# Per-head k-by-v products as 64x64 matmuls on the two column halves of the array, with the short chunk filled up by zeros

## The chip, the core and the metric

The kernel runs on one core of one Trainium2 chip. The time is the device time of one execution in microseconds (us); the kernel before was run three times, and one further execution was profiled. PE is TensorE (the matmul engine), PEld its weight loads, DVE the vector engine, ACT the scalar engine, POOL GpSimd, and SP the engine whose queue issues all of this kernel's DMAs.

## What is computed

The program joins linear attention with two feed-forward blocks. Batch is 8, there are 8 heads of width 64 and 576 rows in a sequence, all in float32:

```python
kv  = np.einsum('bhsd,bhse->bhde', k, v)          # 64x64 for each batch and head
out = np.einsum('bhsd,bhde->bhse', q, kv)
out = out / sqrt(mean(out * out, axis=-1) + 1e-6) * g_norm
x   = out, heads side by side                      # 4608 x 512
x   = (s * relu(x @ w_in)**2 + b) @ w_out          # d_ff 2048
y   = max(x @ w1, x @ w2, x @ w3) @ w_out2         # d_ff 768
```

The change concerns only the first line, `kv`.

## The kernel before

Heads are handled in pairs: `p` counts the four pairs of a batch `bb`, so there are 32 products of k by v. A pair's k is 128 columns wide (64 for each head), and so is its v. The 576 rows are cut into four full chunks of 128 rows and one short chunk of 64 (`NC = 4`, `REM = 64`). `s1` multiplies the whole 128x128 k-by-v product for each chunk (L201 for the full ones, L202 for the short one), accumulated in one PSUM tile `kvps`, and then copies only the two 64x64 blocks on the diagonal out, one for each head: by L207 for the first two batches (`EARLY`), by `hilo` (L82 on ACT, L83 on DVE) into `kvbd` for the other six. The operands are plain float32, and the trace shows two weight loads and two matmuls for each matmul call: 256 of L201 for 32 x 4 calls, 64 of L202 for 32.

`load_kv` fetches a pair's four full chunks (`kv`, two buffers in pool `kvp`) and the short one (`kvr`, a single buffer in pool `kvrp`). Batch 0 takes its tiles from the weight pool instead, with one load for the short chunks of all four pairs. Loads run two pairs ahead of `s1` (`kv_ahead`).

After `s1` of a pair come `s2` (the split of q into two float32r parts), `s3` (q times kv, L226 or L231), and `s4` (norm and the writing of the activations `xh`, `xl`). The first feed-forward block (`u1` L313, `u2` L336) runs in 'slots', a column block of 128 of the 2048 at a time for a tile of 512 tokens; the steps `s1` to `s4` of the next tokens are spread evenly between the slots (`todo`, `beside`). Its partial sums go out to DRAM (`y_dr`). The second block (`v1` L377, `v2` L396) follows after all of that. Weights are taken apart on ACT and DVE (`w_float`, `w_parts`), mostly in the first 200 us. A list scheduler turns this program order into the order on each engine.

A few small constants (`g_sb`, `sb_sb`, `lnb`, `exb`) stand in four tiles of their own; L491 to L513 fill them at the start.

Of the kernel before, what the change touches and what calls it, by code (L numbers as in the profile page):

```python
# [7 lines left out]
F32 = mybir.dt.float32  # L8
# [3 lines left out]
ALU = mybir.AluOpType  # L12
# [7 lines left out]
P = 128  # L20
# [3 lines left out]
def fused_kernel(ctx, tc, qt, kv, kvr, g_norm, w_in, w_out, s, b, w1, w2, w3, w_out2, out):  # L24
    nc = tc.nc
    B, NP, SM, _, _ = kv.shape
    REM = kvr.shape[2]
    S = SM + REM
    D = g_norm.shape[0]
# [8 lines left out]
    NC = SM // P  # L38
# [6 lines left out]
    def pool(name, bufs, space=None):  # L45
        kw = {"space": space} if space is not None else {}
        return ctx.enter_context(tc.tile_pool(name=name, bufs=bufs, **kw))

    const = pool("const", 1)
    wp = pool("wp", 2 * KF)  # L50
# [5 lines left out]
    wt1 = pool("wt1", 2)  # L56
    gp1 = pool("gp1", 1)
    kvp = pool("kvp", 2)
    kvr_p = pool("kvrp", 1)
    qp = pool("qp", 2)  # L60
    ap2 = pool("ap2", 2)
    ap1 = pool("ap1", 1)
# [6 lines left out]
    EARLY = 2  # L69
    start = [wp.tile([P, NP + 2, P], F32, tag="w", name=f"start{i}") for i in range(EARLY)]  # L70
    onesf, zero = start[0][:, NP, :], start[0][:, NP + 1, :]
    g_sb = const.tile([P, 1], F32, name="g_sb")
    sb_sb = const.tile([P, 2], F32, name="sb_sb")
    lnb = const.tile([P, 1], F32, name="lnb")
    exb = const.tile([P, 1], F32, name="exb")
    kvbd = [const.tile([P, 2, P], F32R, name=f"kvbd{p}") for p in range(NP)]
    y_dr = [dram.tile([P, KD, TW], F32, name=f"y_dr{t}") for t in range(NTILE)]

    dma = nc.sync.dma_start

    def hilo(hi, lo, src, eng):
        nc.scalar.activation(out=hi, in_=src, func=ACTF.Copy)  # L82
        eng.tensor_tensor(out=lo, in0=src, in1=hi.bitcast(F32), op=ALU.subtract)  # L83


    def w_load(src):
# [18 lines left out]
    def w_parts(bf, nm):  # L105
        t = wp.tile([P, 2, DM], F32R, tag="w", name=nm)
        with tc.high_priority(60):
            hilo(t[:, 0, :], t[:, 1, :], bf, nc.vector)
        return t

    class Weights:
# [11 lines left out]
        def to(self, cnt):  # L123
            cnt = min(cnt, len(self.need))
            while self.done < cnt:
                self.load(self.half + 3)
                if self.half < len(self.need):
                    self.f32[self.half] = w_float(self.raw.pop(self.half))
                    self.half += 1
                if self.done < self.half - 1 or self.half == len(self.need):  # L130
                    _, d, key = self.need[self.done]
                    d[key] = w_parts(self.f32.pop(self.done), f"w{self.done}")
                    self.done += 1
# [4 lines left out]
    def stage():  # L138
        return stp.tile([P, DM], F32, tag="st", name="st")


    kv_t, krem, q_t = {}, {}, {}

    def load_kv(bb, p):
        first = bb == 0
        pl, tg = (wp, "w") if first else (kvp, "kv")
        t = pl.tile([P, NC, 2, P], F32, tag=tg, name="kv")
        dma(out=t, in_=kv[bb, p].rearrange("(p c) z d -> p c z d", c=NC))
        kv_t[bb, p] = t
        if not first:  # L150
            t = kvr_p.tile([REM, 2, P], F32, tag="kvr", name="kvr")
            dma(out=t, in_=kvr[bb, p])
            krem[bb, p] = t
        elif p == 0:
            t = wp.tile([REM, NP, 2, P], F32, tag="w", name="kvr")
            dma(out=t, in_=kvr[0].rearrange("n p z d -> p n z d"))
            for i in range(NP):
                krem[0, i] = t[:, i]

    def load_q(it):  # L160
        bb, pc, p = it
# [13 lines left out]
    def temps(it, nm):  # L175

        n = PIECES[it[0]][it[1]][1] - PIECES[it[0]][it[1]][0]
        if it[0] >= EARLY:
            pl, dt, tg = TEMPS[nm]
            return pl.tile([P, PW], dt, tag=tg, name=nm)[:, :n]  # L180
        return tmp_t[it][:, HEADS[nm], :n]
# [8 lines left out]
    def bank(bb, i, nm):  # L190
        if bb > 0:
            return ps_a.tile([P, TW], F32, tag="a", name=nm)
        pl, tg = ((ps_y, f"y{i % 4}"), (ps_h, "h"), (ps_a, "a"))[("kvps", "ops", "mps").index(nm)]
        return pl.tile([P, TW], F32, tag=tg, name=nm)

    def s1(bb, p):
        t = kv_t.pop((bb, p))
        r = krem.pop((bb, p))
        ps = bank(bb, p, "kvps")
        for c in range(NC):  # L200
            nc.tensor.matmul(ps[:, :P], lhsT=t[:, c, 0, :], rhs=t[:, c, 1, :], start=(c == 0), stop=False)  # L201
        nc.tensor.matmul(ps[:, :P], lhsT=r[:, 0, :], rhs=r[:, 1, :], start=False, stop=True)  # L202
        t = kvbd[p]
        for j in range(2):
            r = slice(j * D, (j + 1) * D)
            if bb < EARLY:
                nc.vector.tensor_copy(start[bb][:, p, :][r, r], ps[r, r])  # L207
                continue
            hilo(t[r, 0, r], t[r, 1, r], ps[r, r], nc.vector)

    qT_t, o_t = {}, {}

    def s2(it):
        if it[0] < EARLY:
            return
        t = q_t.pop(it)
        qh, ql = temps(it, "qh"), temps(it, "ql")
        hilo(qh, ql, t, nc.vector)
        qT_t[it] = (qh, ql)

    def s3(it):
        bb, pc, p = it
        n = PIECES[bb][pc][1] - PIECES[bb][pc][0]
        ps = bank(bb, p, "ops")[:, :n]
        if bb < EARLY:
            nc.tensor.matmul(ps, lhsT=start[bb][:, p, :], rhs=q_t.pop(it), start=True, stop=True)  # L226
        else:
            qh, ql = qT_t.pop(it)
            w = kvbd[p]
            for i, (l, r) in enumerate(((w[:, 0, :], qh), (w[:, 0, :], ql), (w[:, 1, :], qh))):  # L230
                nc.tensor.matmul(ps, lhsT=l, rhs=r, start=(i == 0), stop=(i == 2))  # L231
        sq, og = temps(it, "sq"), temps(it, "og")
        nc.scalar.activation(out=sq, in_=ps, func=ACTF.Square)
        if bb < EARLY:
            if bb == 0:
                nc.scalar.activation(out=og, in_=ps, func=ACTF.Copy, scale=g_sb)
            else:
                nc.vector.tensor_scalar(out=og, in0=ps, scalar1=g_sb, scalar2=None, op0=ALU.mult)
            o_t[it] = (og, sq, None)
            return  # L240
        nc.scalar.activation(out=og, in_=ps, func=ACTF.Copy, scale=g_sb)
        sh, sl = temps(it, "sh"), temps(it, "sl")
        hilo(sh, sl, sq, nc.vector)
        o_t[it] = (og, sh, sl)

    x_t = {}
# [2 lines left out]
    def x_tile(i):  # L249
        if i not in x_t:  # L250
            x_t[i] = (
                xp.tile([P, KD, TW], F32R, tag="xh", name="xh"),
                xp.tile([P, KD, TW], F32R, tag="xl", name="xl"),
            )
        return x_t[i]

    def put_x(p, g0, src, n):
        xh, xl = x_tile(g0 // TW)
        o = g0 % TW
        hilo(xh[:, p, o:o + n], xl[:, p, o:o + n], src, nc.vector)  # L260

    def s4(it, limit):
        bb, pc, p = it
# [88 lines left out]
    y_t, h2t, acc = {}, {}, {}  # L352

    def y_load(t, j):
        if t not in y_t:
            y_t[t] = (
                xp.tile([P, KD, TW], F32R, tag="xh", name="yh"),
                xp.tile([P, KD, TW], F32R, tag="xl", name="yl"),
            )
        st = stage()  # L360
        dma(out=st, in_=y_dr[t][:, j, :])
        hilo(y_t[t][0][:, j, :], y_t[t][1][:, j, :], st, nc.vector)

    rot = [0]

    def v1(t, m):
        yh, yl = y_t[t]
        a1 = gp1.tile([P, TW], F32, tag="g", name="a1")
        for j in range(3):
            pl, tg = ((ps_h, "h"), (ps_a, "a"))[rot[0] % 2]  # L370
            rot[0] += 1
            h = pl.tile([P, TW], F32, tag=tg, name="h2ps")
            w = wb[m, j].rearrange("p z (a c) -> p z a c", c=P)
            i = 0
            for kk in range(KD):
                for z, x in ((0, yh), (0, yl), (1, yh)):
                    nc.tensor.matmul(h, lhsT=w[:, z, kk, :], rhs=x[:, kk, :], start=(i == 0), stop=(i == 3 * KD - 1))  # L377
                    i += 1
            if j == 0:
                nc.scalar.activation(out=a1, in_=h, func=ACTF.Copy)  # L380
            else:
                nc.vector.tensor_tensor(out=a1, in0=h, in1=a1, op=ALU.max)  # L382
        hh = gp.tile([P, TW], F32R, tag="gh", name="hh")
        hl = gp.tile([P, TW], F32R, tag="gl", name="hl")
        hilo(hh, hl, a1, nc.vector)
        h2t[t, m] = (hh, hl)

    def v2(t, m):
# [46 lines left out]
    def do_s1(it):  # L435
        s1(it[0], it[2])
        done["kv"] += 1
        kv_ahead(done["kv"] + 2)
# [36 lines left out]
    for t in range(HEAD, NTILE):  # L475
        first = max(i for i, sl in enumerate(slots) if sl[0] == t - 2) + 1
# [19 lines left out]
    for j in range(2):  # L496
        r = slice(j * D, (j + 1) * D)
# [28 lines left out]
    for i, sl in enumerate(slots):  # L526
        t, o, n, f, fa, fb = sl
# [96 lines left out]
```

## Time and profile before

| | us |
|---|---|
| median of 3 runs | 1516.36 |
| the 3 runs | 1515.51, 1516.36, 1520.39 |
| the profiled execution, its own time | 1515.98 |
| its span from first to last instruction | 1514.2 |
| PE busy | 1487.5 |
| DVE busy | 717.0 |
| ACT busy | 559.0 |

The profile is of one execution. 1.8 us of its time lie outside the span. Busy time of PE is the union of matmul durations that overlap one another, so what one matmul costs is read from the distance of its start to the next one's start, and not from its own duration.

### The profile page before, as it was taken

What the parts mean: (1) busy time and instruction counts of PE and PEld (TensorE: products, weight loads), DVE (VectorE), ACT (ScalarE), POOL (GpSimd) and SP (SyncE); (2) the same over time, 40 slices, a digit from 0 to 9 for tenths busy, and PEclk for the clock granted to TensorE, in tenths of its full rate; (3) what the DMA queues carried; (4) which work ended last, traced back from release to release, by engine and by line L of the source; (5) the groups of instructions that cost most, each with busy time, mean ns of one, the idle gap of its engine ahead of it and who ended that gap; (6) DMA issues with size and microseconds to landing.
All of it is one profiled execution on the core that took longest, in us unless ns stands there. A gap on an engine that the chain in (4) does not pass through costs nothing.

```text
span 1514.2 us, 17497 instructions
## 1 busy us (share of the span) xinstructions
PE 1487.5 (98%) x6744; PEld 1228.9 (81%) x6744; DVE 717.0 (47%) x1369; ACT 559.0 (37%) x1134; POOL 2.2 (0%) x12
## 2 busy tenths in 40 slices
PE   7799999999999999999999999999999999999999
PEld 5678878888888888888888887888888888888887
DVE  5999976344444454544459783222222212222122
ACT  5665456344444454554555442121211212112111
POOL 0000000000000000000000000000000000000000
PEclk9999999999999999999999999999999999999999
DMA  6555542001111111110104442010110101011000
GB/s 200 174 182 180 177 147 76 25 24 54 43 47 52 40 45 58 30 55 29 42 14 149 144 132 63 0 56 1 56 56 0 56 1 56 14 43 56 1 29 28
DMA packets 47395, 99.70 MB, mean 66 GB/s; under 512 B 5840, under 2 KB 16080, under 8 KB 47312
## 3 DMA queue, kind: packets, MB, share of 16 engines
q1 hardware_dynamic: 47312, 98.59, 20.6%
q8 instruction: 53, 0.87, 0.2%
q14 instruction: 30, 0.25, 0.0%
HBM read 73.40 MB, written 25.17 MB: 65 GB/s over the span
## 4 chain that ended last, share of the span: by engine, by line
PE 89%; DVE 5%; DMA 3%; ACT 2%; issue 1%; SPq 0%; DVEq 0%; ACTq 0%
PE h2ps L377 29%; PE h L313 22%; PE y L336 22%; PE o L396 10%; PE kvps L201 2%; PE ops L231 1%; DMA raw<-in_w_out 1%; DMA raw<-in_w_in 1%; PE kvps L202 1%; DVE tb L100 1%; PE mps L269 1%; DVE w L83 1%; DVE r L323 1%; DVE gl L325 1%; DVE st L342 0%
## 5 line engine op out<-in xcount | busy, mean ns | idle before, releaser
L377 PE MATMUL h2ps<-yh,w 128*128 128x512 f32 x1296 | 407.7, 389 | 1.8 <-ACT yh L82 1.8
L313 PE MATMUL h<-xh,w 128*128 128x512 f32 (+1 forms) x1176 | 386.2, 389 | 3.8 <-ACT xh L82 3.6
L336 PE MATMUL y<-gh,w 128*128 128x512 f32 (+1 forms) x1176 | 385.0, 389 | 0.7 <-ACT gh L324 0.4
L377 PEld LDWEIGHTS h2ps<-yh,w 128*128 128x128 f32 x1296 | 243.1, 188 | 52.7 <-ACT yh L82 2.2
L313 PEld LDWEIGHTS h<-xh,w 128*128 128x128 f32 x1176 | 221.1, 189 | 51.2 <-ACT xh L82 6.5
L336 PEld LDWEIGHTS y<-gh,w 128*128 128x128 f32 x1176 | 220.1, 188 | 47.3 <-ACT gh L324 0.9
L377 PE MATMUL h2ps<-yl,w 128*128 128x512 f32 x648 | 252.1, 389 | 0.0
L382 DVE TENSOR_TENSOR a<-h2ps,a 128x512 f32<-128x512 f32 x108 | 74.6, 691 | 361.9 <-PE h2ps L377 361.7
L313 PE MATMUL h<-xl,w 128*128 128x512 f32 (+1 forms) x588 | 229.3, 390 | 0.9 <-DVE xl L83 0.9
L336 PE MATMUL y<-gl,w 128*128 128x512 f32 (+1 forms) x588 | 227.6, 388 | 0.0
L323 DVE SCALAR_TENSOR_TENSOR r<-r,sb_sb 128x512 f32<-128x512 f32 (+1 forms) x147 | 108.7, 739 | 132.2 <-ACT r L322 131.6
L325 DVE SCALAR_TENSOR_TENSOR gl<-r,sb_sb,gh 128x512 fp32r<-128x512 f32 (+1 forms) x147 | 108.7, 739 | 131.0 <-ACT gh L324 128.8
L324 ACT ACTIVATE gh<-r,sb_sb 128x512 fp32r<-128x512 f32 (+1 forms) x147 | 104.9, 713 | 146.8 <-PE y L336 136.9
L322 ACT ACTIVATE r<-h 128x512 f32<-128x512 f32 (+1 forms) x147 | 86.5, 588 | 169.6 <-PE h L313 146.8
L377 PEld LDWEIGHTS h2ps<-yl,w 128*128 128x128 f32 x648 | 121.7, 188 | 25.4 <-DVE yl L83 0.2
L82 ACT ACTIVATE hh<-a 128x512 fp32r<-128x512 f32 x54 | 34.1, 632 | 268.3 <-DVE a L382 268.3
L396 PE MATMUL o<-w,hh 128*128 128x512 f32 x432 | 133.0, 389 | 0.0
L313 PEld LDWEIGHTS h<-xl,w 128*128 128x128 f32 x588 | 111.3, 189 | 22.8 <-DVE xl L83 1.7
L336 PEld LDWEIGHTS y<-gl,w 128*128 128x128 f32 x588 | 110.5, 188 | 19.8
L380 ACT ACTIVATE a<-h2ps 128x512 f32<-128x512 f32 x54 | 32.3, 598 | 190.6 <-PE h2ps L377 190.6
L396 PEld LDWEIGHTS o<-w,hh 128*128 128x128 f32 x432 | 81.0, 188 | 16.8
L396 PE MATMUL o<-w,hl 128*128 128x512 f32 x216 | 84.0, 389 | 0.0
(77 smaller groups left out, 1120.7 us busy)
## 6 DMA issues: line engine op xcount, KB each, us to landing
kv<-in_kv SPq DMA_DIRECT2D x32, 512.0 KB, 4.0
st<-y_dr SPq DMA_DIRECT2D x60, 256.0 KB, 4.3
y_dr<-st SPq DMA_DIRECT2D x56, 256.0 KB, 3.0
raw<-in_w_out SPq DMA_DIRECT2D x22, 512.0 KB, 3.6
raw<-in_w SPq DMA_DIRECT2D x18, 512.0 KB, 3.5
out<-st SPq DMA_DIRECT2D x36, 256.0 KB, 2.0
raw<-in_w_in SPq DMA_DIRECT2D x16, 512.0 KB, 3.7
qt<-in_qt SPq DMA_DIRECT2D x28, 160.0 KB, 2.2
```

The lines of the kernel that those rows point to most:

```text
L82: nc.scalar.activation(out=hi, in_=src, func=ACTF.Copy)
L201: nc.tensor.matmul(ps[:, :P], lhsT=t[:, c, 0, :], rhs=t[:, c, 1, :], start=(c == 0), stop=False)
L313: nc.tensor.matmul(h[:, :n], lhsT=w[:, z, kk, :], rhs=x[:, kk, o:o + n], start=(i == 0), stop=(i == 3 * KD - 1))
L322: nc.scalar.activation(out=rn, in_=h[:, :n], func=ACTF.Relu)
L323: nc.vector.scalar_tensor_tensor(out=rn, in0=rn, scalar=sb_sb[:, 0:1], in1=rn, op0=ALU.mult, op1=ALU.mult)
L324: nc.scalar.activation(out=gh[:, :n], in_=rn, func=ACTF.Identity, bias=sb_sb[:, 1:2])
L325: nc.vector.scalar_tensor_tensor(out=gl[:, :n], in0=rn, scalar=sb_sb[:, 1:2], in1=gh[:, :n].bitcast(F32), op0=ALU.add, op1=ALU.subtract)
L336: nc.tensor.matmul(yt[t, o][j][:, :n], lhsT=w[:, z, c], rhs=r[:, :n], start=(f == fa and i == 0), stop=(f == fb - 1 and i == 2))
L377: nc.tensor.matmul(h, lhsT=w[:, z, kk, :], rhs=x[:, kk, :], start=(i == 0), stop=(i == 3 * KD - 1))
L380: nc.scalar.activation(out=a1, in_=h, func=ACTF.Copy)
L382: nc.vector.tensor_tensor(out=a1, in0=h, in1=a1, op=ALU.max)
L396: nc.tensor.matmul(acc[t][j], lhsT=l[:, c], rhs=w[:, z, :], start=(m == 0 and i == 0), stop=(m == KM - 1 and i == 2))
```

## The change

Each matmul call of `s1` on a 128x128 block becomes two calls on 64x64 blocks, one for each head `j`: weights `t[:, 0, d]`, moving data `t[:, 1, d]`, output `ps[d, d]` with `d` the 64 columns of the head. Output partitions 0 to 63 belong to the first 64 columns of the array and 64 to 127 to the other 64. The short chunk is held in a fifth chunk of the same `kv` tile, whose lower 64 partitions GpSimd sets to zero, so that its matmuls too contract over 128 rows. The pool `kvrp` goes, and the short chunk has as many buffers as the rest of its tile. The four tiles of constants become columns of one tile. `hilo` loses an argument that was the same engine everywhere.

```diff
-    kvr_p = pool("kvrp", 1)
...
-    g_sb = const.tile([P, 1], F32, name="g_sb")
-    sb_sb = const.tile([P, 2], F32, name="sb_sb")
-    lnb = const.tile([P, 1], F32, name="lnb")
-    exb = const.tile([P, 1], F32, name="exb")
+    cst = const.tile([P, 8], F32, name="cst")
+    g_sb, sb_sb, lnb, exb = cst[:, 0:1], cst[:, 1:3], cst[:, 3:4], cst[:, 4:5]
...
     def load_kv(bb, p):
-        first = bb == 0
-        pl, tg = (wp, "w") if first else (kvp, "kv")
-        t = pl.tile([P, NC, 2, P], F32, tag=tg, name="kv")
-        dma(out=t, in_=kv[bb, p].rearrange("(p c) z d -> p c z d", c=NC))
-        kv_t[bb, p] = t
-        if not first:
-            t = kvr_p.tile([REM, 2, P], F32, tag="kvr", name="kvr")
-            dma(out=t, in_=kvr[bb, p])
-            krem[bb, p] = t
-        elif p == 0:
-            t = wp.tile([REM, NP, 2, P], F32, tag="w", name="kvr")
-            dma(out=t, in_=kvr[0].rearrange("n p z d -> p n z d"))
+
+        if bb > 0:
+            t = kvp.tile([P, NC + 1, 2, P], F32, tag="kv", name="kv")
+            nc.gpsimd.memset(t[REM:, NC], 0.0)
+            dma(out=t[:, :NC], in_=kv[bb, p].rearrange("(p c) z d -> p c z d", c=NC))
+            dma(out=t[:REM, NC], in_=kvr[bb, p])
+            kv_t[bb, p] = [t[:, c] for c in range(NC + 1)]
+            return
+        t = wp.tile([P, NC, 2, P], F32, tag="w", name="kv")
+        dma(out=t, in_=kv[0, p].rearrange("(p c) z d -> p c z d", c=NC))
+        if p == 0:
+            r = wp.tile([P, NP, 2, P], F32, tag="w", name="kvr")
+            nc.gpsimd.memset(r[REM:], 0.0)
+            dma(out=r[:REM], in_=kvr[0].rearrange("n p z d -> p n z d"))
             for i in range(NP):
-                krem[0, i] = t[:, i]
+                krem[i] = r[:, i]
+        kv_t[0, p] = [t[:, c] for c in range(NC)] + [krem.pop(p)]
...
     def s1(bb, p):
-        t = kv_t.pop((bb, p))
-        r = krem.pop((bb, p))
+        rows = kv_t.pop((bb, p))
         ps = bank(bb, p, "kvps")
-        for c in range(NC):
-            nc.tensor.matmul(ps[:, :P], lhsT=t[:, c, 0, :], rhs=t[:, c, 1, :], start=(c == 0), stop=False)
-        nc.tensor.matmul(ps[:, :P], lhsT=r[:, 0, :], rhs=r[:, 1, :], start=False, stop=True)
+        for c, t in enumerate(rows):
+            for j in range(2):
+                d = slice(j * D, (j + 1) * D)
+                nc.tensor.matmul(ps[d, d], lhsT=t[:, 0, d], rhs=t[:, 1, d], start=(c == 0), stop=(c == NC))
```

## Rows read from the trace of the kernel before

**Rows 1.** Page, part 1: busy us, share of span, instructions.

```profile
PE 1487.5 (98%) x6744; PEld 1228.9 (81%) x6744; DVE 717.0 (47%) x1369; ACT 559.0 (37%) x1134; POOL 2.2 (0%) x12
```

**Rows 2.** Windows: stretch, length, busy PE, PEld, DVE, ACT, POOL, clock, DMA share, GB/s.

```profile
0.00:20.00 20.00, 13.08 (x50) 10.51 (x50) 5.95 (x20) 5.98 (x14) 2.17 (x12) 1.00 0.83 273
20.00:60.00 40.00, 31.76 (x169) 25.28 (x170) 35.97 (x94) 27.94 (x69) 0.00 (x0) 0.87 0.48 146
60.00:83.70 23.70, 19.17 (x97) 14.01 (x96) 22.39 (x59) 18.25 (x47) 0.00 (x0) 1.00 0.55 160
83.70:211.30 127.60, 126.16 (x567) 104.09 (x565) 119.90 (x233) 66.61 (x119) 0.00 (x0) 1.00 0.56 181
211.30:720.00 508.70, 508.66 (x2379) 422.37 (x2380) 244.81 (x488) 244.73 (x548) 0.00 (x0) 1.00 0.15 47
720.00:1514.00 794.00, 788.71 (x3489) 652.61 (x3487) 287.98 (x479) 195.50 (x338) 0.00 (x0) 1.00 0.15 48
```

**Rows 3.** Page, part 4: the chain that ended last, shares by line.

```profile
PE h2ps L377 29%; PE h L313 22%; PE y L336 22%; PE o L396 10%; PE kvps L201 2%; PE ops L231 1%; DMA raw<-in_w_out 1%; DMA raw<-in_w_in 1%; PE kvps L202 1%; DVE tb L100 1%; PE mps L269 1%; DVE w L83 1%; DVE r L323 1%; DVE gl L325 1%; DVE st L342 0%
```

**Rows 4.** Tile kvps, 199 to 720 us: duration ns min/median/max, first and last start.

```profile
L201 PE MATMUL kvps<-kv x176: 270/275/377, 199.4 to 716.5; 128*128 128x128 f32 x176
L202 PE MATMUL kvps<-kvr x44: 272/322/373, 200.3 to 716.9; 64*128 64x128 f32 x44
```

**Rows 5.** Timeline of PE around one product: start us, us, engine, line.

```profile
699.67 0.39 PE L336 MATMUL y<-gh,w 128*128 128x512 f32 x1
699.89 1.05 PE L201 MATMUL kvps<-kv 128*128 128x128 f32 x8
700.88 0.48 PE L202 MATMUL kvps<-kvr 64*128 64x128 f32 x2
701.29 0.50 PE L313 MATMUL h<-xh,w 128*128 128x512 f32 x1
701.63 0.40 PE L313 MATMUL h<-xl,w 128*128 128x512 f32 x1
```

**Rows 6.** Timeline of the weight loads (PEld) around the same product.

```profile
699.67 1.08 PEld L201 LDWEIGHTS kvps<-kv 128*128 128x128 f32 x8
700.88 0.29 PEld L202 LDWEIGHTS kvps<-kvr 64*128 64x128 f32 x2
701.29 0.19 PEld L313 LDWEIGHTS h<-xh,w 128*128 128x128 f32 x1
```

**Rows 7.** Timeline of PE: matmuls of 256 and of 512 columns.

```profile
709.99 0.28 PE L231 MATMUL ops<-ql,kvbd 128*128 128x256 f32 x1
710.11 0.28 PE L231 MATMUL ops<-qh,kvbd 128*128 128x256 f32 x1
710.23 0.40 PE L336 MATMUL y<-gh,w 128*128 128x512 f32 x1
710.47 0.40 PE L336 MATMUL y<-gl,w 128*128 128x512 f32 x1
```

**Rows 8.** Waits of PE: total us, times, longest.

```profile
PE kvps L201 <- ACT og L241: 1.5, 1, 1.5
PE kvps L202 <- DMA kvr<-in_kvr: 0.6, 1, 0.6
```

**Rows 9.** Chain in order of time, first 92 us: start, us, what.

```profile
10.12 1.71 PE kvps L201 x8
11.82 0.74 PE kvps L202 x2
...
52.94 4.40 DMA kvr<-in_kvr
...
60.70 0.41 PE kvps L202 x2
...
81.16 0.89 PE kvps L201 x8
```

**Rows 10.** Groups by line, GpSimd's and the vector engine's fills: busy, mean ns.

```profile
L504 POOL CAST kvbd<-start 128x128 fp32r<-128x128 f32 x8 | 2.0, 298 | 1.3 <-DVE start L495 1.3
...
L495 DVE MEMSET start<- 128x768 f32 x2 | 1.4, 698 | 0.2
```

**Rows 11.** Timeline of SP's queue, 684 to 702 us.

```profile
685.10 0.33 SPq L148 DMA_DIRECT2D kv<-in_kv  x1
685.53 0.47 SPq L152 DMA_DIRECT2D kvr<-in_kvr  x1
701.39 0.47 SPq L152 DMA_DIRECT2D kvr<-in_kvr  x1
```

More of the change, by code (lines that the diff above doesn't have):

```diff
@@ L79, in fused_kernel, with hilo @@
     dma = nc.sync.dma_start
-    def hilo(hi, lo, src, eng):
+    def hilo(hi, lo, src):
         nc.scalar.activation(out=hi, in_=src, func=ACTF.Copy)
-        eng.tensor_tensor(out=lo, in0=src, in1=hi.bitcast(F32), op=ALU.subtract)
+        nc.vector.tensor_tensor(out=lo, in0=src, in1=hi.bitcast(F32), op=ALU.subtract)
     def w_load(src):
@@ L107, in w_parts @@
         with tc.high_priority(60):
-            hilo(t[:, 0, :], t[:, 1, :], bf, nc.vector)
+            hilo(t[:, 0, :], t[:, 1, :], bf)
         return t
@@ L208, in s1 @@
                 continue
-            hilo(t[r, 0, r], t[r, 1, r], ps[r, r], nc.vector)
+            hilo(t[r, 0, r], t[r, 1, r], ps[r, r])
     qT_t, o_t = {}, {}
@@ L217, in s2 @@
         qh, ql = temps(it, "qh"), temps(it, "ql")
-        hilo(qh, ql, t, nc.vector)
+        hilo(qh, ql, t)
         qT_t[it] = (qh, ql)
@@ L242, in s3 @@
         sh, sl = temps(it, "sh"), temps(it, "sl")
-        hilo(sh, sl, sq, nc.vector)
+        hilo(sh, sl, sq)
         o_t[it] = (og, sh, sl)
@@ L259, in put_x @@
         o = g0 % TW
-        hilo(xh[:, p, o:o + n], xl[:, p, o:o + n], src, nc.vector)
+        hilo(xh[:, p, o:o + n], xl[:, p, o:o + n], src)
     def s4(it, limit):
@@ L361, in y_load @@
         dma(out=st, in_=y_dr[t][:, j, :])
-        hilo(y_t[t][0][:, j, :], y_t[t][1][:, j, :], st, nc.vector)
+        hilo(y_t[t][0][:, j, :], y_t[t][1][:, j, :], st)
     rot = [0]
@@ L384, in v1 @@
         hl = gp.tile([P, TW], F32R, tag="gl", name="hl")
-        hilo(hh, hl, a1, nc.vector)
+        hilo(hh, hl, a1)
         h2t[t, m] = (hh, hl)
```

## The prediction

> **What bounds the kernel now.** I read the busy shares first: PE is busy 98% of the span, the vector engine 47% [rows 1]. A share hides stages, so the windows come next [rows 2]. The reader is to see two kernels in one. Up to 83.7 us PE idles 6.9 + 8.2 + 4.5 = 19.7 us, while the vector engine is busy 35.97 of 40 us and 22.39 of 23.7 us: weights are being taken apart, and a PE that gets faster there mostly waits longer. From 83.7 us on PE has no gaps but 1.4 us near 211, where a product waits for a PSUM buffer that the scalar engine must empty [rows 8], and 5.3 us from 720 on. There a microsecond of PE time saved or added is a microsecond of the kernel. The chain of waits agrees: matmul lines carry it, and 3% of it is the products of k by v themselves, L201 and L202 [rows 3].
>
> Where the 32 products lie decides what they are worth. 22 of them stand between 199 and 717 us (176 matmuls of L201 at 8 a product, 44 of L202 at 2) [rows 4]. Of the other ten, the first eight are through at 61 us and the last two begin at 81 us [rows 9], where PE becomes the bound. So 24 count in full.
>
> **What one product costs.** The timeline of PE around one of them [rows 5] gives it. The first matmul of L201 starts at 699.89, the next other matmul at 701.29: 1.40 us. That next one is shown 0.10 us longer (0.50) than its neighbours (0.40), because its weight load, which starts at the same 701.29 [rows 6], isn't hidden. So a product holds PE for 1.50 us. Inside, eight matmuls take 1.05 us with a last one of 0.275 us [rows 4, 5], so they start 0.775 / 7 = 0.111 us apart. Ten at that distance would be 1.11 us. The remaining 0.39 us is the short chunk: its 64 rows use half the height of the array, and both on the way in and on the way out PE lets the running matmul finish, loads weights in the open (0.10 us) and only then goes on. That is 0.195 us a switch.
>
> **The change, part by part.** It removes the 64-row matmuls, and with them these two switches: 0.39 us a product. It adds a stretch on half-width pieces of the array with a way in and a way out. The trace shows no half-width matmul, so that pair of switches costs between nothing and 0.39 us. I take 0.39, the nearest row, since here too the shape in which the array is used changes. The Trainium skill (TensorEngine Tiling (Array Packing), section Key Properties) says the same: a change of tiling mode, though not of the tile within a mode, drains the engine. The rows on the 64-row matmuls agree with its first half, at 0.195 us a drain; by it the switches stay at 0.39 us.
>
> Each product goes from 10 pairs of load and matmul to 20, each with half the weight columns and half the moving columns. Matmul time goes with the columns: 256 columns are 0.12 us apart (709.99, 710.11, 710.23), 512 are 0.24 [rows 7], and the 128-column float32 pieces cost 0.111, close to the 256. Half of that is 0.056 us for a 64-column piece. If the halves of the array work one after the other, 20 x 0.056 = 1.12 us, and nothing is won. If they work side by side, the issue order of a chunk (two pieces of head 0, two of head 1) lets the second piece of one head run beside the first of the other: ten steps of 0.056 and one for the ends, 11 x 0.056 = 0.61 us. In between or beyond lies the weight load. Every load here starts when the matmul ahead of it starts (0.00 to 0.02 us later) [rows 5, 6], and in the open it takes 0.10 us for 128 columns. Today it hides exactly under a 0.111 us matmul; under one of 0.056 us it hides only if it halves too, or if the other half's matmul covers it. So a piece costs 0.030 us (side by side) to 0.10 us (load in the open). The present 0.111 lies beyond; it would need a cost that doesn't shrink with the columns. I take the 0.030: the load is already started early, and the two heads touch disjoint weights, columns and output partitions, so no row of the trace gives a reason for one to wait for the other.
>
> The sum: 0.61 + 0.39 = 1.00 us against 1.50, so 0.50 us a product; 24 x 0.50 = 12.0 us. For the first eight: three run slowly enough that eight matmuls take 1.71 us [rows 9], 0.214 apart, and would save up to 1.07 us each, the other five 0.50: 5.7 us at most, nothing at least. With the vector engine at 90% and more after 20 us I take a quarter, 1.5 us.
>
> The rest I cost at nothing. The zero fill of 28 short chunks (64 x 256) lies between the 0.30 us cast of 128 columns on GpSimd and twice that [rows 10]; GpSimd is otherwise idle after 20 us [rows 2], and a tile is requested long before it is used (the load issued at 685.10 [rows 11] serves the product whose last matmuls start at 716.9 [rows 4]). Without that cover it would be up to 0.6 us a product. The first fill (64 x 1024) is 0.9 us by the vector engine's memset, 2.4 by eight casts' worth of columns; its chunk is needed after the four full ones, at 7.4 us. The copies into `kvbd` behind it on GpSimd serve batch 2. The short chunk's load used to wait for its only buffer: the full chunks of one product are asked for at 685.10, its short chunk only at 701.39, when the product at 699.89 is through [rows 11]. Now it follows its full chunks at once, so what is behind it on SP's queue no longer waits for a product, and the one product that waited 0.6 us for it [rows 8] after a 4.40 us transfer [rows 9] may not. Those 0.6 us sit in the stretch where PE idles anyway: 0 to 0.6, taken as 0. The constants in one tile change no instruction; should dependences go by the tile, the first norm waits for two small loads, under 1 us. Copies out of PSUM keep their shape. `hilo` emits the same instructions.
>
> Total: 12.0 + 1.5 = 13.5 us off the profiled 1515.98, so 1502.5 us. The profiled execution stands 0.4 us below the median, so I hold this against the median too.
>
> **The rivals.** *One half after the other* (the change doesn't do what it says): 1.12 + 0.39 = 1.51 us, 1516 us; with free switches 1.12, which is 9 us off, 1507. For it: one moving stream fed the array in every row. The break-even piece is (1.50 - 0.39) / 20 = 0.0555 us.
>
> *The weight load in the open* (slower side): a load that starts with the matmul before it and takes 0.05 to 0.10 us for 64 columns makes a piece 0.08 in the middle: 20 x 0.08 + 0.39 = 1.99 us, 24 x 0.49 = 12 us more, 1528 us; at 0.10 us 2.39, 21 us more, 1537. It decides against the change as soon as a piece exceeds 0.0555 us. For it: the start times of the loads. Against it: loads hide fully today.
>
> *Halves that serialise altogether*: if each of the 9 changes of head between chunks and within them costs a switch of 0.195 us, a product takes 1.12 + 0.39 + 1.76 = 3.27 us, 1558 us. The Trainium skill (TensorE: Matmul & The Clock Gate, Part 3: Packing small matmuls — row/col tiling) points that way: it lets a weight load overlap matmuls in flight only when their row groups differ, and two column halves share all their rows. The loads that start with a full-height matmul on the same rows [rows 5, 6] disagree with it for the whole array; by that rule a piece would be 0.10 + 0.056 us and the product 3.5 us, about 1564.
>
> **How the numbers follow.** Side by side 0.48 (1502.5, or 1493 with free switches; up to 1511 where a piece takes 0.046). One after the other 0.22, of which 0.06 with free switches. Load in the open 0.18. Serialised 0.12. Within 0.3%, 4.5 us, a measurement can't tell it from no change. Faster: 0.48 + 0.06 = 0.54. Same: 0.16 and the 0.02 of the loads that are offset by free switches, 0.18. Slower 0.28. The range goes from 1492 (free switches) to 1534 (a piece of 0.09 us) and leaves out the serialised case and the worst loads. For the likeliest case alone it is 1492 to 1511.
>
> **What the profile would show.** Right: about 640 matmuls in `s1`, overlapping, 20 of them in some 0.6 to 0.7 us, and 1.0 us from the first to the one after the product. The switches: the next matmul's load in the open, as now. The rivals: start distances of 0.056, 0.08 to 0.10, or a 0.2 us hole at each change of head. Wrong altogether it would be if PE waited for GpSimd's fill, if the early stretch grew, or if the scheduler reordered the steps so that the PSUM wait near 211 us grew.

## The result and the profile after

The changed kernel took 1502.09 us (median of 4 runs, 1499.33 to 1504.31) against 1516.52 us before (median of 4): a ratio of 0.9899, 95% interval 0.9875 to 0.9923, 14.4 us faster. Run again beside later experiments it gave 0.9886 (0.9866 to 0.9907). Its profiled execution, the fastest of the four, took 1499.33 us with a span of 1497.5; that is 16.7 us less than the profiled execution of the kernel before (1515.98). The runs of one kernel differ along with their mean granted clock: 0.997 in this fastest run, 0.993 in the slowest.

The page's busy shares (part 1) and the chain by line (part 4) of the changed kernel:

```profile
PE 1469.7 (98%) x7064; PEld 1207.8 (81%) x7064; DVE 715.3 (48%) x1369; ACT 560.2 (37%) x1134; POOL 11.6 (1%) x41
...
PE h2ps L377 29%; PE h L313 25%; PE y L336 25%; PE o L396 10%; PE ops L231 1%; PE kvps L202 1%; DMA raw<-in_w_out 1%; PE mps L269 0%; DMA kv<-in_kv 0%; PE mps L271 0%; PE mps L272 0%; ACT head L275 0%; DMA st<-y_dr 0%; ACT head L274 0%; DVE tb L97 0%
```

PE has 320 matmuls more than before [rows 1] and 17.8 us less busy time. The products' 3% of the chain [rows 3] are 1% now. The windows, with the columns and the cuts of [rows 2]:

```profile
0.00:20.00 20.00, 11.74 (x97) 8.09 (x97) 8.33 (x26) 7.97 (x20) 3.61 (x15) 1.00 0.87 291
20.00:60.00 40.00, 32.08 (x225) 25.68 (x224) 36.85 (x98) 27.83 (x71) 1.23 (x4) 0.87 0.53 159
60.00:83.70 23.70, 19.12 (x113) 12.76 (x113) 21.79 (x57) 16.81 (x44) 0.61 (x2) 1.00 0.49 146
83.70:211.30 127.60, 126.20 (x595) 104.39 (x595) 119.51 (x231) 68.22 (x123) 0.61 (x2) 1.00 0.58 186
211.30:720.00 508.70, 508.67 (x2631) 418.28 (x2630) 249.95 (x501) 253.72 (x569) 5.53 (x18) 1.00 0.15 45
720.00:1497.00 777.00, 771.93 (x3410) 638.58 (x3409) 278.84 (x459) 185.62 (x314) 0.00 (x0) 1.00 0.15 48
```

From 83.7 us on PE's gaps are as small as before (1.4 us up to 211 us, 5.1 us from 720 on), so what it saves there is time. Before 83.7 us it idles 20.8 us, against 19.7 before, and the vector engine is as busy as it was: by these shares that stretch is still paced by the weights. The timeline of PE around the product that answers to [rows 5]:

```profile
683.97 0.39 PE L336 MATMUL y<-gl,w 128*128 128x512 f32 x1
684.19 0.39 PE L336 MATMUL y<-gh,w 128*128 128x512 f32 x1
684.51 0.80 PE L202 MATMUL kvps<-kv 128*64 128x64 f32 x20
685.24 0.50 PE L313 MATMUL h<-xh,w 128*128 128x512 f32 x1
685.58 0.39 PE L313 MATMUL h<-xl,w 128*128 128x512 f32 x1
685.81 0.40 PE L313 MATMUL h<-xh,w 128*128 128x512 f32 x1
```

and the weight loads there, as in [rows 6], with the vector engine's instruction that the second line names:

```profile
683.97 0.19 PEld L336 LDWEIGHTS y<-gh,w 128*128 128x128 f32 x1
684.51 0.66 PEld L202 LDWEIGHTS kvps<-kv 128*64 128x64 f32 x20 [0.35 <-DVE sl L80]
685.24 0.19 PEld L313 LDWEIGHTS h<-xh,w 128*128 128x128 f32 x1
...
683.79 0.43 DVE L80 TENSOR_TENSOR sl<-sq,sh 128x256 fp32r<-128x256 f32 x1
```

The bracket puts the idle time before the first load down to that instruction. But it was done at 684.22, 0.29 us before the load began, and from 255 us on the same 0.32 us stand between each product and the matmul ahead of it. So the load waited for something else. Ahead of whole pieces it is 0.22 (*Zeros only*, below).

From here on a product's cost is read in the same three pieces: the distance from the matmul ahead of it to its own first, over the usual 0.22; from its first matmul to the next other one; and what that one's distance to its successor has over the usual 0.23. After: 0.32 - 0.22 = 0.10, 685.24 - 684.51 = 0.73, 0.34 - 0.23 = 0.11, together 0.94 us. Before, by [rows 5]: 0, 1.40 and 0.34 - 0.23 = 0.11, together 1.51. So 0.57 us a product, and each product from 255 us on shows the same figures.

Inside, the 20 pieces take 0.80 us with a last one of 0.222 (the tile view below), so the last starts 0.58 us after the first. Read one by one in the trace, the starts come in ten pairs: 0.007 us between the two of a pair, 0.107 us from the first pair to the second, and 0.058 us from each later pair to the next. How many are in flight at one moment shows how they lie: windows of 10 ns on this tile (columns as above, without GpSimd) give eight at a time.

```profile
684.83:684.84 0.01, 0.01 (x8) 0.01 (x4) 0.00 (x0) 0.00 (x0) 1.00 1.15 410
685.00:685.01 0.01, 0.01 (x8) 0.01 (x4) 0.00 (x0) 0.00 (x0) 1.00 0.06 0
```

Pieces of 0.222 us that start one by one 0.058 us apart (as they do in the first experiment) would be four in flight; here there are twice as many. The tile view from 195 to 702 us (duration ns min/median/max; the x147 at its end counts a sample of the 440), PE's waits, GpSimd's groups and SP's queue:

```profile
L202 PE MATMUL kvps<-kv x440: 222/222/270, 196.0 to 700.3; 128*64 128x64 f32 x147
```

```profile
PE kvps L202 <- DMA kv<-in_kv: 5.5, 3, 4.9
...
PE kvps L202 <- ACT og L241: 1.2, 1, 1.2
...
PE kvps L202 <- DMA kvr<-in_kvr: 0.2, 1, 0.2
```

```profile
L145 POOL MEMSET kv<- 64x256 f32 x28 | 8.6, 307 | 658.6 <-PE kvps L202 658.3 <-POOLq L612 0.3
```

```profile
670.12 0.33 SPq L146 DMA_DIRECT2D kv<-in_kv  x1
670.50 0.47 SPq L147 DMA_DIRECT2D kv<-in_kvr  x1
```

No wait of PE is for GpSimd. The fill takes 0.307 us and hides; the load of a product's full chunks waits for it four times, by 0.4 us at most. The short chunk's load follows its full chunks at once, where it used to come 16 us later [rows 11].

### The profile page after: what moved, and what is told of

Its sections match the earlier page's. It is cut to its first block, busy times and chain, and to the rows that moved or that the text cites. A ratio compares the mean times of both kernels' runs of the same rounds, so it can differ in the third digit from the quotient of the medians.

```text
span 1497.5 us, 18228 instructions
## 1 busy us (share of the span) xinstructions
PE 1469.7 (98%) x7064; PEld 1207.8 (81%) x7064; DVE 715.3 (48%) x1369; ACT 560.2 (37%) x1134; POOL 11.6 (1%) x41
## 4 chain that ended last, share of the span: by engine, by line
PE 93%; DVE 2%; ACT 2%; DMA 2%; issue 0%; SPq 0%; ACTq 0%
PE h2ps L377 29%; PE h L313 25%; PE y L336 25%; PE o L396 10%; PE ops L231 1%; PE kvps L202 1%; DMA raw<-in_w_out 1%; PE mps L269 0%; DMA kv<-in_kv 0%; PE mps L271 0%; PE mps L272 0%; ACT head L275 0%; DMA st<-y_dr 0%; ACT head L274 0%; DVE tb L97 0%
## 5 line engine op out<-in xcount | busy, mean ns | idle before, releaser
L323 DVE SCALAR_TENSOR_TENSOR r<-r,cst 128x512 f32<-128x512 f32 (+1 forms) x147 | 108.7, 739 | 130.2 <-ACT r L322 129.4
L325 DVE SCALAR_TENSOR_TENSOR gl<-r,cst,gh 128x512 fp32r<-128x512 f32 (+1 forms) x147 | 108.7, 739 | 125.0 <-ACT gh L324 123.2
L324 ACT ACTIVATE gh<-r,cst 128x512 fp32r<-128x512 f32 (+1 forms) x147 | 105.1, 715 | 139.5 <-PE y L336 129.6
```

The source lines that it names most:

```text
L323: nc.vector.scalar_tensor_tensor(out=rn, in0=rn, scalar=sb_sb[:, 0:1], in1=rn, op0=ALU.mult, op1=ALU.mult)
L324: nc.scalar.activation(out=gh[:, :n], in_=rn, func=ACTF.Identity, bias=sb_sb[:, 1:2])
L325: nc.vector.scalar_tensor_tensor(out=gl[:, :n], in0=rn, scalar=sb_sb[:, 1:2], in1=gh[:, :n].bitcast(F32), op0=ALU.add, op1=ALU.subtract)
```

## The experiments

The first four were run together, with the kernel before beside them (17 runs, 1517.70 us); the last three together likewise (17 runs, 1520.05 us). The kernel before moves by 3.5 us between sessions, so ratios are compared and not times.

**The two heads in turn.** Only the order of the calls changes:

```diff
-        for c, t in enumerate(rows):
-            for j in range(2):
-                d = slice(j * D, (j + 1) * D)
+        for j in range(2):
+            d = slice(j * D, (j + 1) * D)
+            for c, t in enumerate(rows):
                 nc.tensor.matmul(ps[d, d], lhsT=t[:, 0, d], rhs=t[:, 1, d], start=(c == 0), stop=(c == NC))
```

> The same 20 half-width pieces a product, but all five chunks of head 0 first and then all of head 1, so that neighbours share a half of the array. Theory (two halves work side by side when neighbours are of different halves): pieces one after the other at 0.058 us, the product 0.6 us longer, 24 x 0.58 = 14 us more than the changed kernel, about 1516. Rival (a 64-column piece is cheap by itself, whatever its neighbour): as the changed kernel, 1502.

Measured: 0.9966 (0.9953 to 0.9979), 1513.07 us. The timeline of PE, and windows of 10 ns on the tile (columns as above):

```profile
694.51 0.39 PE L336 MATMUL y<-gh,w 128*128 128x512 f32 x1
694.83 1.20 PE L202 MATMUL kvps<-kv 128*64 128x64 f32 x20
695.95 0.50 PE L313 MATMUL h<-xh,w 128*128 128x512 f32 x1
696.29 0.39 PE L313 MATMUL h<-xl,w 128*128 128x512 f32 x1
```

```profile
695.15:695.16 0.01, 0.01 (x4) 0.01 (x2) 0.00 (x0) 0.00 (x0) 1.00 1.15 410
695.35:695.36 0.01, 0.01 (x6) 0.01 (x6) 0.00 (x0) 0.00 (x0) 1.00 0.00 0
695.70:695.71 0.01, 0.01 (x4) 0.01 (x3) 0.00 (x0) 0.00 (x0) 1.00 0.00 0
```

The same 20 pieces of the same size now lie four deep, and from first to next they take 1.12 us and not 0.73 (the ways in and out, 0.10 and 0.11, are unchanged). So a 64-column piece isn't cheap by itself; it is cheap beside one of the other half. Most of the gain is lost (0.9966 against 0.9899). It is not all lost, as the theory had it (1516): around the change of head six are in flight, so a few pieces still find a partner.

**Zeros only.** The short chunk is filled up, and each chunk is one whole matmul:

```diff
-            for j in range(2):
-                d = slice(j * D, (j + 1) * D)
-                nc.tensor.matmul(ps[d, d], lhsT=t[:, 0, d], rhs=t[:, 1, d], start=(c == 0), stop=(c == NC))
+            nc.tensor.matmul(ps[:, :P], lhsT=t[:, 0, :], rhs=t[:, 1, :], start=(c == 0), stop=(c == NC))
```

> The short chunk filled up with zeros, but whole 128x128 products as before: no half-height and no half-width piece. Theory (the shape of the array's use costs 0.39 us a product before and 0.35 after, ten full pieces 1.11 us): 1.11 us a product against 0.93 in the changed kernel and 1.50 before, so 24 x 0.18 = 4 us slower than the changed kernel, about 1506. Rival (the 0.39 us belongs to the short chunk or to plain float32 as such): 1516, as before.

Measured: 0.9937 (0.9925 to 0.9950), 1508.98 us.

```profile
689.97 0.39 PE L334 MATMUL y<-gh,w 128*128 128x512 f32 x1
690.19 1.27 PE L200 MATMUL kvps<-kv 128*128 128x128 f32 x10
691.23 0.48 PE L311 MATMUL h<-xh,w 128*128 128x512 f32 x1
691.54 0.40 PE L311 MATMUL h<-xl,w 128*128 128x512 f32 x1
```

0, 1.04 and 0.31 - 0.23 = 0.08: 1.12 us, ten pieces and nothing around them, as the theory says. So the filling alone, which takes the half-height matmuls away, gains 0.39 of the 0.57 us, and the halves on top of it bring the other 0.18 after paying for a way in and out of their own.

**Halves, nothing filled.** The short chunk's matmuls contract over 64 rows again:

```diff
-            kv_t[bb, p] = [t[:, c] for c in range(NC + 1)]
+            kv_t[bb, p] = [t[:, c] for c in range(NC)] + [t[:REM, NC]]
```

and both fills go, and batch 0 takes `r[:REM, i]`.

> Halves as in the changed kernel, but the short chunk contracts over its 64 rows, nothing is filled with zeros. Theory: one more change of shape inside each product, 0.15 to 0.2 us, 24 x that = 4 to 5 us more than the changed kernel, 1506 to 1507. Rival (the 64-row piece keeps the mode, the fill buys nothing): 1502.

Measured: 0.9918 (0.9906 to 0.9930), 1505.34 us.

```profile
689.58 0.39 PE L334 MATMUL y<-gh,w 128*128 128x512 f32 x1
689.90 0.95 PE L200 MATMUL kvps<-kv 128*64 128x64 f32 x20
690.78 0.50 PE L311 MATMUL h<-xh,w 128*128 128x512 f32 x1
```

0.88 us where the changed kernel has 0.73, with the same ways in and out, so some 1.08 us a product. The halves alone therefore gain 0.43 of the 0.57 us, and the filling on top of them some 0.15. 24 x 0.15 = 3.6 us; the ratios differ by 0.0019, 2.9 us, with overlapping intervals. In the trace the fill pays; in the time it does so by no more than the runs' scatter.

**Loads only.** Both edits joined: whole matmuls and no filling, with the new buffers, loads and constants.

> Only the loads, buffers and constants of the changed kernel; matmuls whole 128x128, the short chunk over 64 rows as before. Theory (the gain is PE time of the products): 1.50 us a product stays, 1514 to 1517. Rival (the second buffer of the short chunk and the new order of the schedule gave the 3.3 us by which the changed kernel is ahead at its eleventh product): about 1513.

Measured: 0.9994 (0.9985 to 1.0004), 1516.62 us: no difference. A product is as before, 1.39 us from first to next:

```profile
699.06 1.47 PE L198 MATMUL kvps<-kv 128*128 128x128 f32 x10
700.45 0.50 PE L309 MATMUL h<-xh,w 128*128 128x512 f32 x1
```

**Two products in a row.** From batch 2 on `s1` takes two pairs at a time:

```diff
-        s1(it[0], it[2])
-        done["kv"] += 1
+        bb, _, p = it
+        if bb < EARLY:
+            s1(bb, [p])
+            done["kv"] += 1
+        elif p % 2 == 0:
+            s1(bb, [p, p + 1])
+            done["kv"] += 2
```

`s1` puts the second pair's blocks 128 columns further in the same PSUM tile, and copies all four out after the last matmul.

> From batch 2 on, the products of two pairs are put one behind the other into one PSUM tile, so that two products share one way in and one way out (12 of 24 ways are saved). Theory (a way in and out costs 0.34 us): 12 x 0.34 = 4 us less than the changed kernel, about 1498 against 1502. Rival (loads with two buffers then come late, or the doubled copies out of PSUM make PE wait): 1502 or more.

Measured: 0.9852 (0.9833 to 0.9871), 1496.51 us, against 0.9886 (0.9866 to 0.9907), 1501.97 us, of the changed kernel in the same session.

```profile
682.41 0.39 PE L339 MATMUL y<-gh,w 128*128 128x512 f32 x1
682.73 1.39 PE L203 MATMUL kvps<-kv 128*64 128x64 f32 x40
684.04 0.50 PE L316 MATMUL h<-xh,w 128*128 128x512 f32 x1
684.38 0.39 PE L316 MATMUL h<-xl,w 128*128 128x512 f32 x1
```

0.10 + 1.31 + 0.11 = 1.52 us for two products, 0.36 less than twice 0.94. 12 x 0.36 = 4.3 us; the medians differ by 5.5, and its times end (1498.89) below where the changed kernel's begin (1500.47). This version beats both kernels.

**Two ways in and out.** Chunks 0 and 3 whole, the others in halves, accumulated in the same tile:

```diff
+            if c in (0, 3):
+                nc.tensor.matmul(ps[:, :P], lhsT=t[:, 0, :], rhs=t[:, 1, :], start=(c == 0), stop=False)
+                continue
             for j in range(2):
                 d = slice(j * D, (j + 1) * D)
-                nc.tensor.matmul(ps[d, d], lhsT=t[:, 0, d], rhs=t[:, 1, d], start=(c == 0), stop=(c == NC))
+                nc.tensor.matmul(ps[d, d], lhsT=t[:, 0, d], rhs=t[:, 1, d], start=False, stop=(c == NC))
```

> Chunks 0 and 3 of each product as whole 128x128 matmuls, chunks 1, 2 and the short one in halves: the array's use changes four times a product instead of twice. Theory: four whole pieces 0.45, six half steps 0.35, two ways in and out 0.69, together 1.49 us against 0.93, so 24 x 0.56 = 13 us more than the changed kernel, about 1515. Rival (what stands around the halves is the cost of the product, not of a change of shape): 0.45 + 0.35 + 0.34 = 1.14 us, 5 us more, about 1507.

Measured: 1.0004 (0.9991 to 1.0017), 1519.73 us.

```profile
685.51 0.39 PE L316 MATMUL h<-xh,w 128*128 128x512 f32 x1
685.74 0.38 PE L201 MATMUL kvps<-kv 128*128 128x128 f32 x2
686.05 0.45 PE L205 MATMUL kvps<-kv 128*64 128x64 f32 x8
686.43 0.49 PE L201 MATMUL kvps<-kv 128*128 128x128 f32 x2
686.85 0.34 PE L205 MATMUL kvps<-kv 128*64 128x64 f32 x4
687.12 0.50 PE L339 MATMUL y<-gh,w 128*128 128x512 f32 x1
687.45 0.40 PE L339 MATMUL y<-gl,w 128*128 128x512 f32 x1
```

0.01 + 1.38 + 0.10 = 1.49 us, to the digit what the theory adds up. The whole gain is gone. The time is 17.8 us above the changed kernel's of the same session where the theory has 13: the sum counts 24 products and leaves the first eight out. In the two profiled executions, 16.6 us apart, 2.7 us are there by the eleventh product (200.29 against 197.55), where the sum has 1.1 for two products; 13.0 us come between it and the last one (717.36 against 701.58), where it has 11.6 for 21.

**The changed kernel again.**

> The changed kernel once more, beside the others on the same chip, as the yardstick for two products in a row: about 1502 by every theory.

Measured: 0.9886, 1501.97 us, as given above.

## Why the prediction was right

The likeliest case was the one that came: 1502.5 forecast, 1502.09 measured, by the mechanism that it names. That the two lie 0.4 us apart is luck: the forecast saves 13.5 us, the medians differ by 14.4 (11.7 to 19.0 by the interval of the ratio) and the two profiled executions by 16.7, and several terms came out larger than forecast. Step by step:

*Where time counts.* Right. Of the 22 products from 199 us on, the first starts at 199.36 before and at 196.02 after, the last at 715.70 and 699.72. So the stretch between, with 21 products, is 12.6 us shorter. Of that, 0.3 us is the wait for the PSUM buffer near 207 us, 1.2 us where it was 1.5 [rows 8]; the rest is 0.59 a product. No gap of PE took any of the 0.57 back; where the other 0.02 come from isn't shown.

*Side by side.* Right, and shown: turning the order of the calls, with the same pieces, brings 0.39 of the 0.57 us back. The piece was taken at 0.030 us and came to 0.029: from the second pair on, two pieces start every 0.058 us. One after the other, a piece is 0.058 us, which is the forecast 0.056.

*The switches.* Taken at 0.39 a product, the 64-row price; they cost 0.94 - 10 x 0.058 = 0.36. The forecast sign of 1.0 us from the first piece to the matmul behind the product came to 0.73, since 0.10 of the switches lies ahead of the first piece and 0.11 behind the start of that matmul. That they belong to the change of shape, and not to float32 or to the short chunk, is shown from three sides: without any change of shape they are gone (zeros only), shared between two products they are saved once (two products in a row), and doubled they are paid twice (two ways). The rule of the Trainium skill (TensorEngine Tiling (Array Packing), section Key Properties) that a change of mode drains the engine and a change of tile within it does not agrees with all three, and with the 20 pieces that change tiles without a hole.

*The sum of a product.* 1.00 forecast, 0.94 measured, against 1.50 and 1.51 before: 0.50 us saved, and 0.57 it was. Of the 0.06 between forecast and measured, 0.03 is in the pieces (0.61 against 0.58: the step added for the ends isn't there, and a step is 0.058 and not 0.056) and 0.03 in the switch. 24 x 0.57 = 13.7 us for a term put at 12.0.

*The first eight products.* Put at 1.5 us of a possible 5.7. Of the 3.3 us by which the profiled execution is ahead at 199 us, 1.1 belong to the last two of the ten, and 0.5 to the first load's landing (first matmul at 4.92 instead of 5.41), which leaves 1.7. The second profiled execution is ahead by only 1.8 us there, but its first matmul came 0.2 us later than before (5.63), and near 67 us it ran at the half clock, which the other two did not (the rows are at the end). The kernel with the loads alone changed, whose products are as before, is ahead by 0.7 us at the same point (198.69). So part of the 1.7 need not be the products', and the term stays open.

*What was costed at nothing.* Right: the loads, buffers and constants together gave 0.9994, and the fill hides.

*The range.* Its upper end is given as 1534, for a piece of 0.09 us; by the same sum that piece gives 2.19 us a product, 16.6 us more, 1533. Nothing hangs on it.

The rivals: one after the other is what the turned order looks like, and it came near the time it was given. A load in the open shows at the ends alone: 0.05 us between the first pair of pieces and the second (0.107 where the later distance is 0.058) and 0.11 at the way out; nowhere between. Serialised halves are refuted by the eight pieces in flight. The rule cited for that rival (TensorE: Matmul & The Clock Gate, Part 3 of the Trainium skill), that loads overlap matmuls in flight only when row groups differ, doesn't hold here: 20 loads on the same 128 rows lie in 0.66 us beside the 20 matmuls.

## What to carry to other kernels

Where a small matmul sits between large ones, count its changes of array shape before its columns: a way in and out costs 0.36 to 0.39 us here, as much as six or seven paired 64-column steps. Filling a short contraction up with zeros so that its shape doesn't change gains most of what there is by itself (0.39 of 0.57 us), with whole blocks left as they were. The halves gain 0.43 by themselves, so the two overlap, and what one adds depends on whether the other is there. Putting products of a new shape one behind the other saves a way in and out each time. Two column halves give their factor of two only if the calls alternate between them.

## What wasn't expected

The pieces of the two halves don't keep the order of the calls. Each call shows as two matmuls, and a chunk is issued as head 0, head 1, so in strict order the second piece of a product would belong to the same half as the first and start a step after it. The timeline of PE in the changed kernel, cut off at 684.55 us, shows two that start together:

```profile
684.51 0.28 PE L202 MATMUL kvps<-kv 128*64 128x64 f32 x2
```

Both lie within 0.28 us, where one alone takes 0.222 to 0.270. With the heads in turn, strict order would overlap one piece at the change of head, with at most five in flight there; six are. The last piece starts 1.20 - 0.22 = 0.98 us after the first, where strict order has 18 distances of 0.058, 1.04 us, at least. So one half runs some pieces ahead of calls that stand before them in the program, for the other. That is read from starts, counts and sums; the trace doesn't name the half that a matmul used. In the program built from the turned order the five calls of head 0 do stand ahead of the five of head 1, so the list scheduler didn't move them.

From the matmul behind the last product to the end, where the kernels are the same, the profiled execution of the kernel before took 797.1 us (717.10 to 1514.2), that of the changed kernel 797.1 (700.45 to 1497.5), and the second one of the changed kernel 798.7 (702.31 to 1501.0). The second has a stretch there that the first hasn't (windows with the columns of [rows 2], the second execution and then the first):

```profile
913.70:917.00 3.30, 3.30 (x9) 2.62 (x9) 2.33 (x4) 1.93 (x4) 0.00 (x0) 0.50 0.35 87
67.20:70.50 3.30, 3.30 (x13) 2.71 (x12) 2.40 (x6) 2.17 (x6) 0.00 (x0) 0.50 0.45 151
...
913.70:917.00 3.30, 3.30 (x16) 2.70 (x16) 2.69 (x5) 1.16 (x2) 0.00 (x0) 1.00 0.10 34
```

TensorE's granted clock is 0.50 there, 1.2 GHz and not 2.4, and nine matmuls fall into a window that had sixteen. The same holds near 67 us, where the first execution, like the kernel before, has 1.00 in its row from 60 to 83.7 us. A gap of PE of 1.84 us ended at 912.96, just before it; but the first execution has a gap of 1.80 us at 911.06 and keeps its clock; near 67 us a gap of 1.48 us had ended at 66.77. So executions of one kernel differ by 1.6 us in this stretch alone, and the early stretch can differ likewise; single profiles don't settle less than that.
